# Cross-window attention on one core: QK, PV and output projection in 64x64 tiles of TensorE

## The chip, the cores and the metric

The kernel runs on one core of one Trainium2 chip. The core has five engines that run side by side and meet at semaphores: TensorE (matmuls, written PE, and its weight loads, PEld), VectorE (DVE), ScalarE (ACT), GpSimd (POOL) and the sync engine (SP), which here issues all transfers. TensorE writes only to PSUM, which has eight banks of 512 fp32 per partition; VectorE and ScalarE read from there, GpSimd does not. The metric is the time of one execution on the device in microseconds, lower is better, as the median of several runs. A profile of one execution gives the time of every instruction.

## What is computed

The input has 224 x 224 tokens of 96 channels in bf16. The first 48 channels of q, k and v attend within horizontal stripes of 8 rows, the last 48 within vertical stripes of 8 columns. Every stripe is a sequence of 1792 tokens, and there are 28 of each kind.

```python
def reference(x, wqkv, wo):
    B, H, W, C = x.shape                      # 1, 224, 224, 96
    qkv = jnp.einsum('bhwc,cd->bhwd', x, wqkv)
    q, k, v = (qkv[..., :C], qkv[..., C:2 * C], qkv[..., 2 * C:])
    scale = C2 ** (-0.5)                      # C2 = 48
    # horizontal stripes, first 48 channels
    ah = _softmax(jnp.einsum('bqc,bkc->bqk', qh, kh) * scale, axis=-1)
    oh = jnp.einsum('bqk,bkc->bqc', ah, vh)
    # vertical stripes, last 48 channels
    av = _softmax(jnp.einsum('bqc,bkc->bqk', qv, kv) * scale, axis=-1)
    ov = jnp.einsum('bqk,bkc->bqc', av, vv)
    o = concat(oh, ov)
    return jnp.einsum('bhwc,cd->bhwd', o, wo)
```

## The kernel before

Two stripes of one kind make a pair, called P in the code: P = 0 to 13 are horizontal, 14 to 27 vertical. The two stripes of a pair (w = 0, 1) lie on partitions 0 to 63 and 64 to 127. The kernel holds Q and K transposed (channels on partitions, 48 of 64 used) and V with tokens on partitions and a column of ones behind the 48 channels, so that PV also gives the sum of the row. A row's maximum is not taken; the mean of K over the stripe is subtracted instead, which changes nothing in the softmax.

**Loads and fills.** `load(P)` (L383) puts x transposed into one of two buffers `xT_sb`: a horizontal stripe is one transposing DMA, a vertical one is eight of 224 tokens, so a vertical P takes 16. A buffer is free when all the fills of the P two before have read it. `prep(P)` (L478) projects it in 12 fills: K and Q in four chunks of 512, 512, 512 and 256 tokens, V in two parts for each stripe. A fill is a matmul group into one PSUM bank and a VectorE evacuation (L518 for K with its sum, L513 for Q, L555 for V); GpSimd subtracts the mean of K (L529). The fills of P + 1 are spread over the time of P.

**Units.** For every P and every chunk of 512 queries there are 14 key tiles of 128 tokens (7 double tiles for the chunk of 256). Such a unit is QK (L708): two matmuls, one for each stripe, 48 rows by 128 columns by 512, side by side in the two row halves of the array, each into a bank of its own. So a unit is a 128 x 1024 tile of scores in a pair of banks. Of 49 units of a P, 41 go to ScalarE, which takes the exponential of the tile in one instruction (L726, into one of eight buffers `PT`). The other 8 go to VectorE, which builds the exponential from the bits of the exponent in four instructions: I (L750, from PSUM), U (L756), E (L758) and G (L760); their product is a sum of two terms, E and G, so such a unit has two PV. PV (L691) is two matmuls for each unit, 128 rows by 64 columns by 512, one for each stripe, side by side in the two column halves of the array, added up over the key tiles in one bank.

**Banks.** Banks 0 to 5 are a ring of three pairs for scores. Banks 6 and 7 are accumulators for PV, taken by whichever chunk comes next. A fill or a projection takes one bank: a half of a ring pair, or an accumulator that is free (`FillPool`, L309).

**The end of a chunk.** VectorE copies the accumulator to `OT_sb` (L655), and `fin` (L565) projects it with `wo`: 128-row matmuls against a `wo` with zeros in the rows of the other stripe (L583 horizontal, L612 vertical). VectorE takes the reciprocal of the sum (L571) and multiplies: a horizontal result is kept in `Ph_sb` (L590), a vertical one goes to `tmp` (L619), GpSimd adds the horizontal part (L623), and four or two tiles for each stripe are stored, 28 stores in all for a P (L632).

**The order.** A planner in the kernel (`Planner`, L76) places all operations on all engines by its own table of costs and writes each engine's program in that order; each engine's program, the queue of SP included, is then fixed. `pick_pe` (L148) chooses TensorE's next operation. A change between the shape of the QK tiles and that of all others is a change of TensorE's mode. A wait that is late at the head of an engine's program holds all that stands behind it.

## Time and profile before

| | |
|---|---|
| median of 3 runs | 1107.05 us (1104.41 to 1108.44) |
| the profiled execution | 1103.27 us |
| its span, first to last instruction | 1101.5 us |
| mean granted clock of TensorE | 0.989 |
| exponentials on ScalarE (L726) | 1148, 1059.3 us busy |
| units on VectorE (L750) | 224 |
| stores / transposing loads of x | 392 / 252 |

How to read the views. A group line gives the source line, the engine, the operation, the tiles written and read with their shape, the count, then the busy time, the mean duration of one in ns, the idle time of the engine just before such instructions and what ended it. In the timeline a row has start, length, engine, line, operation and count, and in brackets the idle time before it and its releaser. "SPq" rows are the issue of transfers by the sync engine. "issue" as a releaser means that the profile shows nothing that the engine waited for; waits for a transfer appear so. Instructions of one engine overlap in part, so a mean duration is longer than the distance from one to the next.

### The profile page before, as it was taken

Reading aid. Unit: us, or ns where it says so; the run is one execution under the profiler, and the core shown is the slowest. Engines: PE = TensorE matmul, PEld = TensorE weight load, DVE = VectorE, ACT = ScalarE, POOL = GpSimd, SP = SyncE. Lnnn points to the kernel's source line nnn. Section 1 sums busy time; section 2 is a strip of 40 time slices with the busy share of each in tenths; the row PEclk is TensorE's granted clock in tenths of the full one; section 3 lists DMA queues with packets and bytes.
Section 4 is the critical chain, followed back from the end, with each engine's and each line's share of the span. In section 5 each row is a group of like instructions: output and inputs, shape, how many; then the busy total and the mean of one; then the engine's idle time right before and its main releaser. Section 6 shows DMA issues by size and latency. Waiting matters only on the chain.

```text
span 1101.5 us, 24997 instructions
## 1 busy us (share of the span) xinstructions
PE 1046.9 (95%) x10424; PEld 386.4 (35%) x10424; DVE 949.9 (86%) x1941; ACT 1062.8 (96%) x1154; POOL 153.3 (14%) x143
## 2 busy tenths in 40 slices
PE   7999999999999999999999999999999999989996
PEld 2333333333333333333333333333333333323332
DVE  5899889889888998898899889988988978868876
ACT  4999999999999999999999999999999989979996
POOL 0000000000000000000022122222221222212221
PEclk9999999999999999999999999999999989989998
DMA  5101201110121012011112222222222222222110
GB/s 104 35 1 35 35 9 27 35 35 1 35 35 34 1 35 35 3 33 29 20 29 42 39 41 42 39 41 43 40 41 42 41 39 43 40 39 42 37 29 19
DMA packets 168904, 37.05 MB, mean 34 GB/s; under 512 B 168792, under 2 KB 168792, under 8 KB 168792
## 3 DMA queue, kind: packets, MB, share of 16 engines
q1 hardware_dynamic: 168792, 35.47, 17.5%
q8 instruction: 81, 1.33, 0.5%
q14 instruction: 31, 0.25, 0.1%
HBM read 0.10 MB, written 9.63 MB: 9 GB/s over the span
## 4 chain that ended last, share of the span: by engine, by line
ACT 63%; PE 17%; DVE 17%; issue 1%; DMA 0%; POOL 0%; POOLq 0%; SPq 0%
ACT PT L726 63%; PE ps L708 8%; PE ps L691 7%; DVE I_sb L750 5%; DVE G_sb L760 4%; DVE KT_sb L518 2%; DVE U_sb L756 2%; DVE E_sb L758 1%; DVE OT_sb L655 1%; PE ps L499 1%; PE ps L583 1%; DVE QT_sb L513 1%; DVE Ph_sb L590 1%; DMA xT_sb<-in_x_dram 0%; PE ps L612 0%
## 5 line engine op out<-in xcount | busy, mean ns | idle before, releaser
L726 ACT ACTIVATE PT<-ps 128x1024 bf16<-128x1024 f32 x1148 | 1059.3, 1107 | 20.8 <-PE ps L708 20.1
L708 PE MATMUL ps<-QT_sb,KT_sb 48*128 48x512 bf16 (+1 forms) x3136 | 490.9, 360 | 25.4 <-ACT PT L726 16.0
L691 PE MATMUL ps<-PT,V_sb 128*64 128x512 bf16 (+1 forms) x2576 | 447.6, 371 | 0.3 <-ACT PT L726 0.3
L750 DVE TENSOR_SCALAR I_sb<-ps 128x1024 int16<-128x1024 f32 x224 | 273.4, 1221 | 42.7 <-PE ps L708 37.7
L708 PEld LDWEIGHTS ps<-QT_sb,KT_sb 48*128 48x128 bf16 x3136 | 125.1, 93 | 327.8 <-ACT PT L726 195.6
L691 PEld LDWEIGHTS ps<-PT,V_sb 128*64 128x64 bf16 x2576 | 134.1, 108 | 170.4 <-issue 160.4
L760 DVE TENSOR_TENSOR G_sb<-I_sb,U_sb 128x1024 bf16<-128x1024 bf16 x224 | 176.9, 790 | 3.3
L623 POOL TENSOR_TENSOR out_sb<-tmp,Ph_sb 128x384 bf16<-128x384 f32 (+1 forms) x112 | 99.8, 896 | 414.4 <-DVE tmp L619 338.9
L529 POOL TENSOR_SCALAR KT_sb<-KT_sb,negmean 128x1792 bf16<-128x1792 bf16 x27 | 53.3, 1976 | 529.8 <-DVE kjunk L523 529.7
L756 DVE TENSOR_SCALAR U_sb<-I_sb 128x1024 int16<-128x1024 int16 x224 | 96.5, 431 | 2.0
L691 PE MATMUL ps<-G_sb,V_sb 128*64 128x512 bf16 (+1 forms) x560 | 91.1, 356 | 5.7 <-DVE G_sb L760 4.9
L499 PE MATMUL ps<-xT_sb,w_sb 96*64 96x512 bf16 x448 | 84.4, 379 | 11.1 <-issue 10.8
L758 DVE TENSOR_SCALAR E_sb<-I_sb 128x1024 int16<-128x1024 int16 x224 | 92.7, 414 | 0.0
L691 PE MATMUL ps<-E_sb,V_sb 128*64 128x512 bf16 (+1 forms) x560 | 89.6, 350 | 1.5 <-DVE E_sb L758 0.9
L518 DVE TENSOR_SCALAR_CACHE_REDUCE KT_sb<-ps 128x512 bf16<-128x512 f32 x112 | 68.3, 618 | 22.2 <-PE ps L499 22.0
L555 DVE CAST V_sb<-ps 128x480 bf16<-128x480 f32 x112 | 53.8, 501 | 38.2 <-PE ps L550 37.3
L513 DVE TENSOR_SCALAR QT_sb<-ps 128x512 bf16<-128x512 f32 x108 | 66.9, 619 | 18.2 <-PE ps L499 18.1
L655 DVE CAST OT_sb<-ps 128x512 bf16<-128x512 f32 x112 | 69.3, 618 | 6.8 <-PE ps L691 6.8
L619 DVE TENSOR_TENSOR tmp<-ps,rc 128x384 f32<-128x384 f32 (+1 forms) x112 | 56.3, 502 | 1.0
L590 DVE TENSOR_TENSOR Ph_sb<-ps,rc 128x384 bf16<-128x384 f32 x98 | 54.1, 552 | 0.6
L691 PEld LDWEIGHTS ps<-G_sb,V_sb 128*64 128x64 bf16 x560 | 27.0, 108 | 56.1 <-DVE G_sb L760 39.2
L571 DVE RECIPROCAL rc<-ps 128x4 f32<-128x4 f32 (+1 forms) x210 | 36.3, 173 | 10.3 <-PE ps L612 10.3
(28 smaller groups left out, 281.6 us busy)
## 6 DMA issues: line engine op xcount, KB each, us to landing
out_dram<-out_sb SPq DMA_DIRECT2D x392, 24.0 KB, 1.9
xT_sb<-in_x_dram SPq DMA_TRANSPOSE x252, 2.5
wo_sb<-in_wo_dram SPq DMA_DIRECT2D x4, 9.0 KB
wo_sb<-one_sb SPq DMA_DIRECT2D x4, 0.0 KB
w_sb<-in_wqkv_dram SPq DMA_DIRECT2D x1, 54.0 KB, 2.5
xT_sb<-in_x_dram SPq DMA_DIRECT2D x2, 3.0 KB, 3.9
```

The lines of the kernel that those rows point to most:

```text
L499: ins = e.matmul(bk[64 * w:64 * w + 64, 0:qs], lhsT=w_sb[0:C, wblk(P, kind), :], rhs=rhs, start=True, stop=True)
L513: return e.tensor_scalar(dst, src, A128, None, ALU.mult)
L518: return e.tensor_scalar(KT_sb[b][:, q0:q0 + qs], bk[:, 0:qs], 1.0, None, ALU.mult, ALU.add, accum_out=ksum[b][:, c:c + 1])
L623: return e.tensor_tensor(out_sb[b][:, w, g[0]:g[0] + n, :], tmp[hold[1].tok["t"]][:, 0:n, :], Ph_sb[:, g[0]:g[0] + n, j, :], ALU.add)
L655: return e.tensor_copy(OT_sb[b][:, q0:q0 + qs], bk[:, 0:qs])
L691: ins = e.matmul(bank(k.bank)[64 * w:64 * w + 64, 0:qs], lhsT=lhs(w, kt), rhs=rhs(w, i, qs), start=(op.tok["first"] and i == 0), stop=(k.l ...
L708: ins = e.matmul(bank(2 * s + w)[:, i * qs:(i + 1) * qs], lhsT=KT_sb[b][64 * w:64 * w + C2, kt * 128:(kt + 1) * 128], rhs=QT_sb[b][64 * w: ...
L726: a.fn = lambda e: e.activation(PT[a.tok["p"]][:].rearrange("p (s n) -> p s n", s=2), two(q.tok["s"]), ACTF.Exp, scale=LN128)
L750: d.fn = lambda e: e.tensor_scalar(I_sb[d.tok["y"]][:, :].rearrange("p (s n) -> p s n", s=2), two(q.tok["s"]), 128.0 * ONE, 0.0, ALU.add, ...
L756: f.fn = lambda e: e.tensor_scalar(U_sb[d.tok["y"]][:, :], I_sb[d.tok["y"]][:, :], M_FRAC, HALF, ALU.bitwise_and, ALU.bitwise_or)
L758: x2.fn = lambda e: e.tensor_scalar(E_sb[x2.tok["l"]][:, :], I_sb[d.tok["y"]][:, :], M_EXP, E_LOW, ALU.bitwise_and, ALU.bitwise_or)
L760: g.fn = lambda e: e.tensor_tensor(G_sb[x2.tok["l"]][:, :], I_sb[d.tok["y"]][:, :].bitcast(BF16), U_sb[d.tok["y"]][:, :].bitcast(BF16), AL ...
```

## The change

Two pairs, P = 2g and 2g + 1, now run side by side as the two lanes of a group g; there are 14 groups.

- QK is in 64 x 64 tiles: a unit has 64 keys of both stripes of both pairs against 512 queries of each, so four matmuls, which take the four quarters of the array. Lane p has bank p of the ring pair. PV is in 64 x 64 tiles as well, and so is the output projection, which now needs only the 49 rows of its own stripe (`wo_sb` has no zero half any more). The tile of a unit is 128 x 1024 as before.
- Each lane has an accumulator bank of its own, 6 or 7. The lanes go through their chunks in different orders (`ORDER`), so that one is at a chunk's end 14 units before the other; both end together at a group's end. Where one lane is in its chunk of 256 queries, the unit has six matmuls.
- A group has 98 units, 16 of them on VectorE, evenly spread (`dset`); 82 go to ScalarE.
- A fill or a projection takes a whole ring pair and is evacuated two banks at once: K in two fills of 896 tokens, Q in two, V in two, the projection in one for each chunk, up to 768 elements. At the start, K and half of Q of the second pair and half of Q of the first go through ScalarE.
- Q, K and V have four buffers instead of two; `xT_sb` still has two. The output goes through six buffers of one chunk, `tmp` through two.
- The fills of the next group are spread over the whole group, first those of its first pair, then those of the second.
- `pick_pe` is rewritten: there are two modes, the 64 x 64 tiles ("m") and the fills ("f"). At most two ring pairs are held for ScalarE while something else could take the third.

In the built program SP's order in the vertical half is, from the first store on: 12 stores, the 16 loads of P = 18, 32 stores, 16 loads, 24 stores, 16 loads and so on in turn, the 16 of P = 27, then 124 stores.

```diff
-    NKT = NTOK // 128
+    NKT = NTOK // 64
+    ORDER = [(0, 1, 2, 3), (3, 0, 1, 2)]
+    NG = NP // 2
...
-        wo_sb = [[sb(f"wo_sb{v}{w}", [128, C + 1], BF16) for w in range(2)] for v in range(2)]
+        wo_sb = [sb(f"wo_sb{v}", [128, C + 1], BF16) for v in range(2)]
-        QT_sb = [sb(f"QT_sb{i}", [128, NTOK], BF16) for i in range(2)]
-        KT_sb = [sb(f"KT_sb{i}", [128, NTOK], BF16) for i in range(2)]
-        V_sb = [sb(f"V_sb{i}", [128, 2, NKT, CP], BF16) for i in range(2)]
+        QT_sb = [sb(f"QT_sb{i}", [128, NTOK], BF16) for i in range(4)]
+        KT_sb = [sb(f"KT_sb{i}", [128, NTOK], BF16) for i in range(4)]
+        V_sb = [sb(f"V_sb{i}", [128, NKT, CP], BF16) for i in range(4)]
...
-        obanks = Pool([6, 7])
+        obank = [Pool([6]), Pool([7])]
...
     def pick_pe(s, cands):
+        t = s.t["pe"]
+        left = max(s.t["act"], t) + 0.903 * s.pend - t
+        mine = s.pend + sum(1 for f in s.ring.free_by.values() if f and f[0].eng == "act" and f[0].end > t + SLACK)
+        if mine >= MOST and any(q and p in (R_QD, R_FIN, R_FILL) and s.open(q[0]) for p, q in s.streams["pe"]):
+            cands = [c for c in cands if c[1] != R_QA]
+            if not cands:
+                return None
+        elif mine < MOST and any(p == R_QA for _, p, _ in cands):
+            cands = [c for c in cands if c[1] not in (R_QD, R_FIN, R_FILL)]
...
+            dset = {int((i + DOFF) * n / ND) for i in range(ND)}
+            for i, u in enumerate(zip(*lanes)):
+                units.append((g, i, i in dset, u))
...
         def fill(occ, pe_fn, pe_deps, evs, ...):
-            p = Op("pe", occ, occ + 0.18, lambda e: pe_fn(e, bank(p.tok["b"])), pe_deps, soft, [(fills, "b", 1)], mode="v")
+            p = Op("pe", occ, occ + 0.18, lambda e: pe_fn(e, p.tok["s"], p), pe_deps, soft, [(ring, "s", 1)], mode=mode)
...
         def prep(P, pace=None, startup=False):
+            for f in range(2):
+                def pe_fn(e, s, op, f=f):
+                    for i in range(2):
+                        for w in range(2):
+                            t0 = f * HF + i * HB
+                            ins = e.matmul(bank(2 * s + i)[64 * w:64 * w + 64, 0:HB], lhsT=w_sb[0:C, wblk(P, "k"), :],
+                                           rhs=xT_sb[xb][0:C, w, t0:t0 + HB], start=True, stop=True)
+                    return ins
+                def ev_fn(e, s, op, f=f):
+                    dst = KT_sb[b][:, f * HF:(f + 1) * HF].rearrange("p (i n) -> p i n", i=2)
+                    if startup and par:
+                        return e.activation(dst, two(s)[:, :, 0:HB], ACTF.Copy, accum_out=ksum[b][:, f:f + 1])
+                    return e.tensor_scalar(dst, two(s)[:, :, 0:HB], 1.0, None, ALU.mult, ALU.add, accum_out=ksum[b][:, f:f + 1])
...
+            put_q(halves[0], startup)
+            put_v(0)
+            put_v(1)
+            put_q(halves[1], False)
...
         def fin(k):
...
+                ins = e.matmul(bank(2 * s + i)[64 * w:64 * w + 64, j * (C + 1):(j + 1) * (C + 1)],
+                               lhsT=OT_sb[ot][64 * w:64 * w + CA, t0:t0 + 64], rhs=wo_sb[0][64 * w:64 * w + CA, :],
+                               start=True, stop=True)
...
         def pv_op(u, rhs, deps, then):
+            def fn(e):
+                todo = inter([[(k, kts, i, w) for i in range(len(kts)) for w in range(2)] for k, kts in u])
+                for k, kts, i, w in todo:
+                    r = w ^ k.p
+                    ins = e.matmul(bank(6 + k.p)[64 * w:64 * w + 64, 0:k.qs], lhsT=V_sb[k.P % 4][64 * r:64 * r + 64, kts[i], :],
+                                   rhs=rhs()[64 * r:64 * r + 64, k.p * 512 + i * k.qs:k.p * 512 + (i + 1) * k.qs],
+                                   start=(op.tok[k.p] and i == 0), stop=(k.last is op and i == len(kts) - 1))
+                return ins
...
+        def qk_op(u, soft, then):
+                for k, kts, i, w in todo:
+                    r = w ^ k.p
+                    b = k.P % 4
+                    ins = e.matmul(bank(2 * s + k.p)[64 * r:64 * r + 64, i * k.qs:(i + 1) * k.qs],
+                                   lhsT=KT_sb[b][64 * w:64 * w + C2, kts[i] * 64:(kts[i] + 1) * 64],
+                                   rhs=QT_sb[b][64 * w:64 * w + C2, k.q0:k.q0 + k.qs], start=True, stop=True)
...
         prep(0, startup=True)
+        prep(1, startup=True)
+        for g in range(NG):
...
+            if g + 1 < NG:
+                for p in range(2):
+                    load(2 * g + 2 + p, sp_in)
+                def pace():
+                    n = count[0]
+                    count[0] += 1
+                    return [act_of[a_idx[int((n + P0) * len(a_idx) * PACE / 12)]]]
+                for p in range(2):
+                    prep(2 * g + 2 + p, pace=pace)
```

## The prediction

> **What bounds the kernel now.** I read the busy totals first, then who ScalarE waited for by stretch, then the sync engine's queue, then both ends of the run.

> ```profile
> PE 1046.9 (95%) x10424; PEld 386.4 (35%) x10424; DVE 949.9 (86%) x1941; ACT 1062.8 (96%) x1154; POOL 153.3 (14%) x143
> 200.00:400.00 200.00, 193.39 (x1978) 73.46 (x1976) 176.35 (x357) 199.00 (x217) 10.88 (x5) 1.00 0.15 29
> 850.00:1000.00 150.00, 140.54 (x1314) 49.63 (x1312) 124.15 (x261) 138.28 (x150) 33.04 (x34) 0.94 0.21 41
> ```

> Columns of the two stretches: length, busy time of PE, PEld, DVE, ACT, POOL, granted clock, DMA share, GB/s. Two engines look full, but only ScalarE is: 199.00 us for 217 exponentials is 0.917 us each, and 1148 × 0.917 = 1053 us of the 1101.5 us span. TensorE's 95% counts latency and waits; most QK loads wait for an ACT slot (195.6 us on line 726). From 850 us on ScalarE loses 11.7 of 150 us, and the clock drops.

> ScalarE's idle time before L726, asked for 0 to 30 us, 30 to 850 us and 850 us to the end:

> ```profile
> ACT PT L726 <- PE ps L708: 3.7, 6, 1.4
> ACT PT L726 <- PE ps L708: 3.3, 16, 0.3
> ACT PT L726 <- PE ps L708: 13.1, 12, 3.1
> ```

> So 820 us in the middle hold 3.3 us of waiting: nothing done to TensorE or VectorE there can return more. The late 13.1 us have another source, the queue that issues all transfers:

> ```profile
> 583.84 21.42 SPq L397 DMA_TRANSPOSE xT_sb<-in_x_dram  x16
> 605.30 19.40 SPq L632 DMA_DIRECT2D out_dram<-out_sb  x28
> 891.41 16.59 SPq L632 DMA_DIRECT2D out_dram<-out_sb  x24
> 1014.88 84.84 SPq L632 DMA_DIRECT2D out_dram<-out_sb  x96
> 892.66 0.41 PE L499 MATMUL ps<-xT_sb,w_sb 96*64 96x512 bf16 x2 [2.30 <-issue]
> 893.66 1.94 ACT L726 ACTIVATE PT<-ps 128x1024 bf16<-128x1024 f32 x2 [2.24 <-PE ps L708]
> ```

> Columns: start, length, engine. In the vertical half each P needs 16 transposing loads (21.4 us of issuing) and 28 stores at 0.68 us (19.0): 40.4 us, against 41 × 0.917 = 37.6 us of exponentials. The queue falls 2.8 us behind per P, runs without a gap from 583.84 to 1014.88, and near 892 the K fill (L499) waits 2.30 us at the head of TensorE's order for its x. Then matmul pairs come 0.43 us apart instead of 0.22 until about 900 (clock row 0.69 for 890 to 900). The rest follows the queue: the last strip lands near 1017 (1013.49 + 1.34 + 2.4), 82 exponentials remain, 1017 + 75 = 1092, and the last exponential ends at 1093.68.

> **The change part by part.** Work that does not change: 1148 exponentials of 128x1024, 224 units on VectorE, 392 stores, 252 transposes. ScalarE's floor stays 1053 us.

> *Four 64x64 tiles.* A unit is now four matmuls (six where a 256-wide chunk takes part): in the built order 17,144 matmuls instead of 10,424, and 315 changes of tile shape instead of 1,956. No row shows four tiles at once, so bounds. Low 0.22 us per unit, as now; high 0.43, if the pairs run one after the other. What is nearest:

> ```profile
> 301.65 0.60 PE L708 MATMUL ps<-QT_sb,KT_sb 48*128 48x512 bf16 x4
> 316.26 0.64 PE L708 MATMUL ps<-QT_sb,KT_sb 48*128 48x256 bf16 x8 [0.19 <-ACT PT L726]
> 307.90 0.50 PE L550 MATMUL ps<-w_sb,xT_sb 96*64 96x48 bf16 x20
> ```

> The same columns in twice the instructions cost 0.04 us for four more: 0.01 each. I take 0.24 per unit. A change of shape costs 0.09 us (301.34 start of a 64-column pair, 0.22 of streaming, 301.65 the QK). Saved: 1,641 × 0.09 = 148 us; added: 6,720 × 0.01 = 67. Per group (two P, 75.2 us of exponentials): 212 units × 0.24 = 50.9, fills and projections about 7.4, shape changes 2: 60 us. All this lies beside ScalarE: worth 0. At the high end it is 91 + 9 = 100 us per group and the bound: + 25 × 14 = 350 us.

> [...]

> *Wide evacuations.* By shape, 512 to 256 elements is 684 to 419 ns for K (L518), 384 to 192 is 553 to 351 for the product (L619), 480 to 192 is 649 to 352 for V (L555). Continued: K and Q of 896 take 1.08, V of 672 0.85, the product of 768 0.96 us. Against today's counts VectorE saves about 1.7 us of 34 per P. ScalarE's exponentials cover it: worth 0; were VectorE the bound it would be 28 × 1.7 = 48 us.

> *The ring.* Fills lose the half slots and the spare accumulator banks; each takes a whole pair, and ScalarE keeps two of three. The third carries per group: 16 VectorE units (0.42 + 1.22 + 0.1 = 1.74), 8 K/Q fills (0.60 + 1.08 + 0.1), 4 V fills (0.63 + 0.85 + 0.1), 6 wide projections (0.54 + 0.18 + 0.96 + 0.1) and 2 narrow (1.2): 61 us, with 0.2 of queueing on 36 uses 68 us. VectorE's other 30 us (U, E, G, OT) must fit gaps of about 29 us in that loop; if a third doesn't, 78. Bounds 68 and 78 against 75.2. I take a fit, with 2 us lost in the horizontal half, since VectorE is at 88% there now and ScalarE still at 99.5%. One accumulator bank per lane: its 0.69 us evacuation delays the lane's next PV, behind which a QK may stand in TensorE's order; ScalarE holds up to 0.9 us of finished QK, and PV has eight PT buffers: 0. Six output buffers of 9 to 13 us of work each outlast a queue that is 25 us late: 0.

> *Start.* The first unit needs two P.

> ```profile
> 2.18 8.22 SPq L397 DMA_TRANSPOSE xT_sb<-in_x_dram  x4
> 9.20 2.56 PE L499 MATMUL ps<-xT_sb,w_sb 96*64 96x512 bf16 x12 [4.38 <-issue]
> 14.93 1.02 ACT L726 ACTIVATE PT<-ps 128x1024 bf16<-128x1024 f32 x1 [1.36 <-PE ps L708]
> ```

> Issues are 2.05 us apart; the second strip let PE go at 9.20, so the fourth comes near 13.2. Then, at pairs of 0.43: K 0.95, K and Q through ScalarE (0.9 each, in line) to 17.0, V fills in TensorE's order to 17.7, QK 0.65: first exponential 18.3, + 3.4 us. Bounds: +1.5 (strips earlier) and +5.

> *Queue of stores and loads.* The same 80.8 us per group, but a buffer is free 0.60 group (45 us) before its next use, with nothing between the 16 loads. In the new order load 18 can go 33 us into the vertical half, then 10 loads and 256 stores follow without a gap: 214 + 174 = 388, landing 2.5: x of P=27 is there at 423.5. From its place 122 exponentials remain: 112 us, plus 2 for the slow clock: the half takes 537.5. Without that wait, 574 × 0.917 + 2 = 529. Before: 573 exponentials have begun by 548 us and 575 by 550, so the half runs from 549.4 to 1093.7: 544.3. Gain 7. Bounds: 15 (queue keeps up) and −1 (2% slower issuing). It also covers the ring: losses under 8 us in this half vanish behind it.

> *End.* The last two chunks finish together, one 512 wide.

> ```profile
> 1095.14 0.42 DVE L655 CAST OT_sb<-ps 128x256 bf16<-128x256 f32 x1 [0.51 <-PE ps L691]
> 1096.68 1.05 POOL L623 TENSOR_TENSOR out_sb<-tmp,Ph_sb 128x192 bf16<-128x192 f32 x2 [2.59 <-DVE rc L571]
> ```

> From the last exponential: PV 0.45, two OT casts to 1.45, projections, reciprocals and products to 3.3, GpSimd 1.6 (0.55 to 0.91 us for 192 to 384, continued) to 5, then 8 stores × 0.6 behind 4, landing: 12 instead of 7.8. + 4.2, bounds + 2 and + 6.

> **Sum.** 1101.5 + 3.4 + 2 − 7 + 4.2 = 1104, with the 1.8 us outside the span 1106 against that execution's 1103.3. The median of the runs is 3.8 above that execution; I add nothing, since late loads make that scatter and fewer are late: 1106, range of this case 1098 to 1113.

> **Rivals.** *The queue keeps up:* ScalarE never waits for x in the vertical half: 8 us less, 1098; with a start of + 1.5 1096. For it: 45 us of notice instead of 44, less 3 for four stores that no longer split the loads. Against: 5.6 us per group lost over five groups. *The third slot binds:* the loop passes 75.2 us per group; U, E and G run late, G's PV and the next D unit come late, projections pile up, the next group's K is late. At 77 us: 1.8 × 14 = 25, less 8 covered: 1123; at 78, 1137. It decides from about 76. For it: one slot where halves used to overlap. Against: VectorE's total falls. *Tiles run in pairs, not fours:* the change does not do what it says; 1106 + 350.

> **Chances.** About 0.5% is what can be told from no change: faster below 1101.5, slower above 1112.6. Forecast 0.45 (a seventh of it on each outer side), queue keeps up 0.25, third slot 0.25, pairs 0.05. Faster 0.06 + 0.25 = 0.31, slower 0.06 + 0.25 + 0.05 = 0.36, same the remaining 0.33. The range leaves out the fastest ends of the second case and the pairs and worst loops: 1095 to 1130.

> **What would show it.** Right: 0.917 us per exponential between 200 and 400 us; units 0.24 us apart with changes of shape rare; PE busy well down, yet the time unmoved; first exponential near 18.3; the store queue without gaps after the first vertical group; 12 us after the last exponential. [...] Wrong: ScalarE waiting in the horizontal half (ring), or four matmuls starting 0.2 us apart (pairs).

## The result and the profile after

The changed kernel takes 1123.49 us in the median of four runs (1122.51 to 1125.59), the kernel before, on the same chip, 1107.74 us (1104.41 to 1110.67): a ratio of 1.0146, 95% interval 1.0113 to 1.0178. It is slower by about 1.5%; the forecast was 1106 us and no change. The profiled execution took 1122.51 us with a span of 1120.7.

The page of the changed kernel, busy time of each engine and the queue that the page calls instruction (packets, MB, share of the 16 DMA engines' time), and that queue in the page of before:

```profile
PE 970.8 (87%) x17144; PEld 431.6 (39%) x17144; DVE 919.8 (82%) x1522; ACT 1063.0 (95%) x1156; POOL 129.3 (12%) x86
...
q8 instruction: 134, 2.20, 0.8%
...
q8 instruction: 81, 1.33, 0.5%
```

TensorE is busy 76 us less, VectorE 30 less, and ScalarE just as long: the tiles do what they were to do, and what the kernel loses is time in which ScalarE waits. The same two stretches as before, same columns:

```profile
200.00:400.00 200.00, 181.29 (x3234) 81.40 (x3232) 171.50 (x281) 199.71 (x219) 8.79 (x5) 1.00 0.15 27
850.00:1000.00 150.00, 122.24 (x2200) 55.27 (x2196) 115.99 (x190) 133.10 (x144) 25.79 (x17) 0.94 0.22 40
```

In the horizontal half ScalarE does two exponentials more than before in 200 us. In the late stretch it loses 16.9 of 150 us, against 11.7 before. ScalarE's waits for L675 (QK), for 0 to 30 us, 30 to 850 us and 850 us to the end (us in total, times, longest):

```profile
ACT PT L699 <- PE ps L675: 2.9, 4, 1.2
ACT PT L699 <- PE ps L675: 9.9, 3, 9.0
ACT PT L699 <- PE ps L675: 16.6, 7, 8.9
```

Three waits hold nearly all of it: 9.0, 6.4 and 8.9 us, at 818, 904 and 987 us, one a group. The first of them on TensorE and on ScalarE in the timeline:

```profile
816.81 0.39 PE L675 MATMUL ps<-QT_sb,KT_sb 48*64 48x512 bf16 x4
825.76 0.96 PE L442 MATMUL ps<-xT_sb,w_sb 96*64 96x448 bf16 x4 [8.56 <-DMA xT_sb<-in_x_dram]
826.64 0.64 PE L675 MATMUL ps<-QT_sb,KT_sb 48*64 48x512 bf16 x4
827.07 0.64 PE L651 MATMUL ps<-E_sb,V_sb 64*64 64x512 bf16 x4
...
827.34 1.02 ACT L699 ACTIVATE PT<-ps 128x1024 bf16<-128x1024 f32 x1 [8.99 <-PE ps L675]
```

The first K fill of an odd P (L442) stands at the head of TensorE's program and waits 8.56 us for its x; all QK and PV stand behind it. After it the units are 0.43 us apart instead of 0.22 for a while. The queue that issues the transfers, in the vertical half:

```profile
584.30 21.74 SPq L342 DMA_TRANSPOSE xT_sb<-in_x_dram  x16
606.09 24.65 SPq L596 DMA_DIRECT2D out_dram<-out_sb  x32
630.84 22.71 SPq L342 DMA_TRANSPOSE xT_sb<-in_x_dram  x16
653.60 17.23 SPq L596 DMA_DIRECT2D out_dram<-out_sb  x24
...
755.61 23.66 SPq L342 DMA_TRANSPOSE xT_sb<-in_x_dram  x16
...
993.31 17.21 SPq L596 DMA_DIRECT2D out_dram<-out_sb  x26
```

It is full from 584.30 to the end of the last load at 993.3: 409 us for the ten loads and 256 stores that the prediction put at 388. A group of 32 loads and 56 stores takes some 85 us of issuing against 75.7 us of exponentials (82 times 0.923 us, the mean distance in this half without ScalarE's waits). Why issues take longer than they did is to be seen in the chain of waits, where each issue has its own row (start, length, what):

```profile
806.53 1.24 SPq L342
807.77 0.04 issue
807.81 2.15 SPq L342
809.96 0.04 issue
810.00 1.24 SPq L342
...
817.71 1.66 SPq L342
...
823.26 2.41 DMA xT_sb<-in_x_dram
825.67 0.09 issue
825.76 0.96 PE ps L442 x4
```

A load takes 1.24 us to issue, a store 0.60, nearly all alike to a few ns, but some, here called long, take 0.3 to 1.3 us more. The two long ones here lie where the trace has packets of 16,384 bytes on the instruction queue q8, at 807.97 (0.96 us) and 817.38 (0.95). Its packets follow TensorE's program: the 81 in the page of before are 63.7 bytes for each of 20,848 instructions (10,424 matmuls and as many weight loads), the 134 in the page above 64.0 for each of 34,288. From these two counts I estimate that the queue brings TensorE its program, at 64 bytes an instruction, and a packet on it is called a fetch here. With 15,436, 19,888 and 11,992 matmuls, in the runs below, the estimate gives 120.6, 155.4 and 93.7 packets, and their pages count 120, 155 and 94. Between 584 and 1000 us all 31 long issues of the kernel before and 49 of the 50 of the changed one overlap such a fetch in time; the last one starts 0.4 us after a fetch. The other issues are no slower than before.

### The profile page after: what moved, and what is told of

Same layout as the page of the kernel before. It is cut to its first block, busy times and chain, and to the rows that moved or that the text cites. A ratio compares the mean times of both kernels' runs of the same rounds, so it can differ in the third digit from the quotient of the medians.

```text
span 1120.7 us, 37910 instructions
## 1 busy us (share of the span) xinstructions
PE 970.8 (87%) x17144; PEld 431.6 (39%) x17144; DVE 919.8 (82%) x1522; ACT 1063.0 (95%) x1156; POOL 129.3 (12%) x86
## 4 chain that ended last, share of the span: by engine, by line
ACT 66%; issue 10%; DVE 9%; PE 8%; SPq 3%; POOL 2%; DMA 1%; POOLq 0%
ACT PT L699 66%; SPq L342 3%; DVE I_sb L709 3%; PE ps L675 3%; PE ps L651 2%; DVE G_sb L718 2%; POOL out_sb L587 2%; DVE QT_sb L491 1%; PE ps L477 1%; PE ps L442 1%; DMA xT_sb<-in_x_dram 1%; DVE OT_sb L630 1%; DVE U_sb L714 1%; DVE E_sb L716 1%; DVE tmp L584 1%
## 5 line engine op out<-in xcount | busy, mean ns | idle before, releaser
L699 ACT ACTIVATE PT<-ps 128x1024 bf16<-128x1024 f32 x1148 | 1057.7, 1097 | 32.1 <-PE ps L675 29.4
L675 PE MATMUL ps<-QT_sb,KT_sb 48*64 48x512 bf16 (+1 forms) x6272 | 534.0, 364 | 32.6 <-ACT PT L699 16.2
L651 PE MATMUL ps<-PT,V_sb 64*64 64x512 bf16 (+1 forms) x5264 | 440.0, 358 | 52.8 <-ACT PT L699 40.6
L675 PEld LDWEIGHTS ps<-QT_sb,KT_sb 48*64 48x64 bf16 x6272 | 192.7, 105 | 276.4 <-ACT PT L699 203.0
L651 PEld LDWEIGHTS ps<-PT,V_sb 64*64 64x64 bf16 x5264 | 183.0, 106 | 201.9 <-ACT PT L699 157.7
L587 POOL TENSOR_TENSOR out_sb<-tmp,Ph_sb 128x768 bf16<-128x768 f32 (+1 forms) x56 | 83.4, 1489 | 350.4 <-DVE tmp L584 350.4
L651 PE MATMUL ps<-E_sb,V_sb 64*64 64x512 bf16 (+1 forms) x1008 | 90.5, 365 | 8.0 <-DVE OT_sb L630 7.4
L651 PE MATMUL ps<-G_sb,V_sb 64*64 64x512 bf16 (+1 forms) x1008 | 88.1, 358 | 2.9 <-DVE G_sb L718 2.8
L450 DVE TENSOR_SCALAR_CACHE_REDUCE KT_sb<-ps 128x896 bf16<-128x896 f32 x54 | 58.8, 1091 | 37.0 <-PE ps L442 34.0
L630 DVE CAST OT_sb<-ps 128x256 bf16<-128x256 f32 (+1 forms) x112 | 68.1, 618 | 9.2 <-PE ps L651 8.2
L491 DVE TENSOR_SCALAR QT_sb<-ps 128x896 bf16<-128x896 f32 x54 | 58.7, 1086 | 2.9 <-PE ps L477 0.9
L442 PE MATMUL ps<-xT_sb,w_sb 96*64 96x448 bf16 x224 | 34.6, 395 | 28.3 <-DMA xT_sb<-in_x_dram 23.0
```

The lines of the kernel that those rows point to most:

```text
L450: return e.tensor_scalar(dst, two(s)[:, :, 0:HB], 1.0, None, ALU.mult, ALU.add, accum_out=ksum[b][:, f:f + 1])
L491: return e.tensor_scalar(dst, src, A128, None, ALU.mult)
L587: return e.tensor_tensor(out_sb[op.tok["o"]][:, :, 0:n, :], tmp[hold[1].tok["t"]][:, :, 0:n, :], Ph_sb[:, k0:k0 + n, j0:j0 + 2, :].rearran ...
L630: return e.tensor_copy(OT_sb[k.evac.tok["ot"]][:, 0:k.qs], bank(6 + k.p)[:, 0:k.qs])
L651: ins = e.matmul(bank(6 + k.p)[64 * w:64 * w + 64, 0:k.qs], lhsT=V_sb[k.P % 4][64 * r:64 * r + 64, kts[i], :], rhs=rhs()[64 * r:64 * r + 6 ...
L675: ins = e.matmul(bank(2 * s + k.p)[64 * r:64 * r + 64, i * k.qs:(i + 1) * k.qs], lhsT=KT_sb[b][64 * w:64 * w + C2, kts[i] * 64:(kts[i] + 1 ...
```

## The experiments

Theory A: the vertical half is set by SyncE's issue queue, by late x. Theory F, within it: the queue got slower because each fetch of TensorE's program that meets an issue holds it up, and the change has more program. Rival B: the tiles, the ring or the evacuations cost the time. Rival C: not the queue's pace but its order, stores ahead of loads. Spans of the profiled executions: before 1101.5, changed 1120.7 us. Every ratio is to the kernel before on the same chip; a span is that of one execution, and those of the kernel before scatter (its times lie between 1102.2 and 1112.1 us).

**Half of the stores on another queue.** The stores of the second stripe of each pair (w = 1) go to GpSimd's queue: 196 of the 392, all of them in the vertical half, and not 196 in each half as the expectation has it. This is done in the changed kernel, and in the same way in the one before (where a copy into an output buffer then also waits for both queues' stores from it):

```diff
-  dm = Op("sp", 0.06, 2.0, lambda e, w=w, j=j: e.dma_start(...), [op], dma=(s_out[o_], 0))
-  sp_out.append(dm)
+  dm = Op("pool" if w else "sp", 0.06, 2.0, lambda e, w=w, j=j: e.dma_start(...), [op], dma=((s_outp if w else s_out)[o_], 0))
+  (pool_o if w else sp_out).append(dm)
```

> The changed kernel, with the stores of the second sequence of each pair issued by GpSimd's queue instead of SyncE's: 196 in the horizontal half and 196 in the vertical one, under semaphores of their own. Theory A (SyncE's queue bounds the vertical half: 10 transposing loads and some 256 stores take it 409 us, and TensorE waits three times for an x that was issued too late): the three waits of L442 at odd P are gone, ScalarE waits for nothing longer than 1 us between 550 and 1080 us, the vertical half takes 531 to 535 us instead of 558, and the span is 1093 to 1097 us, 24 to 28 less. Theory B (the 64x64 tiles, the ring of banks or the wide evacuations cost the time themselves): the span stays at 1118 to 1122 us.

> The kernel before with the same edit. Theory A: the kernel before also waited for loads in its vertical half, but less: 544 us becomes 531 to 535, and the span 1088 to 1092 us. What is left between this run and the changed kernel with the same edit is then what the tiles, the start and the end cost without the queue: 3 to 9 us by the longer end (12.4 against 7.8 us). Theory B: between the two runs lie the same 16 us as between the two kernels.

Measured: the changed kernel with the edit 1098.53 us, ratio to the kernel before 0.9937 (0.9922 to 0.9952), span 1096.9; the kernel before with the edit 1095.07 us, 0.9906 (0.9891 to 0.9921), span 1093.0. The second is 1 us above the expected 1088 to 1092. ScalarE's waits from 550 to 1080 us, first of the changed kernel with the edit, then of the kernel before with it:

```profile
ACT PT L700 <- PE ps L676: 0.2, 1, 0.2
ACT PT L727 <- PE ps L709: 2.2, 6, 0.5
```

Without the edit they are 26.3 and 12.5 us; the waits for x are gone. The last exponential ends at 1080.4 us in the one kernel and at 1080.2 in the other: with the queue out of the way the two tilings are equal up to there, although the first exponential begins 4.2 us later in the changed one, and B falls. What lies between them, 3.9 us, is the end. Both ends are some 4 to 5 us longer than without the edit (16.5 and 12.8 us), which the next pair of runs takes up.

**The last stores back on SyncE's queue.** As above, but for the last two pairs all stores stay on SyncE's queue (`w and P < NP - 2`).

> The changed kernel with the second sequences' stores on GpSimd's queue except those of the last two pairs, which stay on SyncE's. In the run with all of them on GpSimd's queue, the last exponential ended at 1080.4 and the kernel 16.5 us later, in the changed kernel 12.6 us after it. If GpSimd's queue lengthens the end: 1080.4 + 12.6, span 1092 to 1094 us. If not: 1096 to 1098 us.

> The kernel before with the same edit. Last exponential at 1080.2 with all second stores on GpSimd's queue, and the end 12.8 us after it; in the kernel before the end was 7.8 us after the last exponential. If GpSimd's queue lengthens the end: 1080.2 + 7.8, span 1087 to 1089 us, the fastest of all. If not: 1092 to 1094 us.

Measured: 1094.38 us, ratio 0.9878 (0.9848 to 0.9908), span 1093.3, end 12.6 us; and 1091.31 us, 0.9847 (0.9812 to 0.9883), span 1089.8, end 9.2 us, a little over the 1087 to 1089 expected. So stores on GpSimd's queue lengthen the end. Both are faster than both kernels, and the old tiles with the relieved queue are the fastest: the change still costs its longer end.

**The order of the queue.** The loads' stream stands ahead of the stores' one, and the planner is told the costs of issues.

```diff
-        sp_out, sp_in = (pl.stream("sp", i) for i in range(2))
+        sp_in, sp_out = (pl.stream("sp", i) for i in range(2))
...
+                    op.occ = 2.05 if is_h[P] else 1.35
...
-                        dm = Op("sp", 0.06, 2.0, lambda e, w=w, j=j: ...
+                        dm = Op("sp", 0.7, 2.4, lambda e, w=w, j=j: ...
```

> The changed kernel with the same DMAs on the same queue, but the loads put ahead of the stores where both are due, and the planner told what an issue costs (1.35 us a vertical load, 2.05 a horizontal one, 0.7 a store). Theory A in the form 'the loads stand behind stores that could wait': six output buffers let the stores lag, the loads come in time, and the span is 1094 to 1100 us. Theory A in the form 'the queue has more to issue than time for it': 84 us of issues to a group of 76 us; stores fall back until the output buffers are full, the waits move from x to the output copies, and the span is 1112 to 1122 us. Theory B: 1118 to 1122 us.

> The kernel before with the same edit of order and planned issue costs. It has only two output buffers, so stores can lag by little. If order is what matters: span 1090 to 1096 us. If the queue's throughput is what matters: 1098 to 1106 us, as before.

Measured: the changed kernel 1113.53 us (span 1111.4, 9 less), the kernel before 1118.88 us (span 1116.8, 15 more). No expectation holds to the number: order, with the costs the planner is told, recovers 9 of the 24 us that relief recovers, and in the kernel before it is harmful, which I had not expected. What GpSimd waited for from 550 to 1080 us, first in the changed kernel with the edit (us in total, times, longest):

```profile
POOL out_sb L588 <- DMA out_dram<-out_sb: 95.0, 14, 18.7
```

and in the kernel before with it:

```profile
POOL out_sb L624 <- DMA out_dram<-out_sb: 115.8, 6, 42.4
```

Neither kernel has such a wait without the edit. Stores fall back until the output buffers are full; six of them soften it (ScalarE's longest wait is 4.8 us), two don't (14.3 us). The queue has too much to issue, in whichever order; C is no more than a part.

**More program for TensorE.** An extra matmul of 8 columns, written over by the next one, adds program (155 packets on q8 instead of 134) and little work (2.3 us of span with the relieved queue, see below). It was put into the vertical half, into the vertical half of the version with the relieved queue, and into the horizontal half:

```diff
+                    if i == 0 and k.P >= NPH:
+                        e.matmul(bank(2 * s + k.p)[64 * r:64 * r + 64, 0:8], lhsT=KT_sb[b][...], rhs=QT_sb[b][...], start=True, stop=True)
                     ins = e.matmul(bank(2 * s + k.p)[64 * r:64 * r + 64, i * k.qs:(i + 1) * k.qs],
```

> The changed kernel with one extra matmul of 8 columns in front of each tile's first QK matmul, in the vertical half alone (the real one writes the same place after it): about 2744 matmuls and as many weight loads more, 351 KB of program, which is some 21 more of the 16 KB fetches. Theory F (each fetch of TensorE's program holds up one DMA issue of SyncE by about 0.77 us, and the queue has no time to spare): some 20 fetches lie in the time that the queue sets, so 14 to 17 us more, span 1133 to 1139 us; the long issues between 584 and 1000 us rise from 50 to about 65. Without F, and TensorE 87% busy: 1119 to 1123 us. If the extra TensorE work itself counts, about 0.1 us for each of some 1372 units of exponentials... the same sum would then show in the next run too.

> The same extra matmuls in the changed kernel whose second sequences' stores are issued by GpSimd's queue, where SyncE's queue has time to spare. Theory F: as many more fetches and long issues, but nothing waits for them: span 1096 to 1099 us, as without the extra matmuls (1096.9). If the extra work on TensorE costs by itself, the span rises here as in the run before.

> The changed kernel with the extra matmuls of 8 columns in the horizontal half alone. Theory F: as many more fetches (155 against 134), but in a half in which no load or store is late; only the issues from the 12th group on count: span 1119 to 1124 us, against 1131.9 with the same matmuls in the vertical half. If the matmuls cost by themselves: some 2 to 3 us more, as the run with the relieved queue showed (1099.2 against 1096.9), so 1123 to 1124; if it were any 21 fetches wherever they fall: 1131.

**Less program.** The other direction, with the same transfers. In the vertical half this kernel leaves out PV of one stripe of each pair but for a chunk's first and last tile, so it computes something else:

```diff
                     r = w ^ k.p
+                    if k.P >= NPH and w == 0 and not (op.tok[k.p] and i == 0) and not (k.last is op and i == len(kts) - 1):
+                        continue
                     ins = e.matmul(bank(6 + k.p)...
```

> The changed kernel with part of the computation left out: in the vertical half PV leaves out the first sequence of each pair except the first and the last key tile of a chunk, some 1700 matmuls and weight loads less, 217 KB of program or 13 fetches, and the same DMAs. Theory F: about 12 fewer long issues between 584 and 1000 us, 9 to 10 us off the queue's 409.0 us, waits of ScalarE for x shorter, span 1109 to 1113 us. Without F, and TensorE not the bound: 1119 to 1122 us.

Measured, with the queue's stretch from the first issue of the tenth load from the last to the end of the last one, which is the same 160 load issues and 256 stores in each kernel of this tiling (252 in the kernel before). "Regular" is every issue at 1.241 or 0.598 us, "excess" what the issues take beyond that; the gaps between them, with one short issue of 0.58 us, sum to 19.7 or 19.8 us in all five:

| kernel | fetches on q8 | of them in the stretch | stretch | regular | long issues | excess | span |
|---|---|---|---|---|---|---|---|
| before | 81 | 29 | 390.0 us | 349.3 | 29 | 21.1 us | 1101.5 |
| changed, less program | 120 | 39 | 399.3 | 351.6 | 39 | 27.9 | 1110.7 |
| changed | 134 | 49 | 409.0 | 351.6 | 50 | 37.6 | 1120.7 |
| changed, more in the horizontal half | 155 | 48 | 406.8 | 351.6 | 49 | 35.4 | 1119.3 |
| changed, more in the vertical half | 155 | 64 | 419.4 | 351.6 | 64 | 47.9 | 1131.9 |

The medians are 1113.33 us (less program; ratio 1.0075, 1.0043 to 1.0107), 1122.34 (more, horizontal; 1.0152, 1.0119 to 1.0185) and 1134.6 (more, vertical; 1.0244, 1.0209 to 1.0278), where the changed kernel has 1.0146 (1.0113 to 1.0178). Program added or taken away in the vertical half moves the stretch by +10.4 and −9.7 us and the span by +11.2 and −10.0; the same program in the horizontal half, where no load is late, moves them by −2.2 and −1.4, no more than the spread between executions of one kernel (3.1 us of the changed one). With the relieved queue the extra matmuls cost 2.3 us (median 1100.94 us, span 1099.2 against 1096.9, a little over the 1096 to 1099 expected): where no x is late, their own work costs no more than that. These five kernels agree with F: a long issue costs some 0.75 us, and the stretch changes by the excess and by next to nothing else. The expected 1133 us and more was a little high, since the stretch has 14 long issues more and not 20.

**The same on the kernel before.** An 8-column matmul in front of each QK matmul of its vertical half:

> The kernel before with an extra matmul of 8 columns in front of each QK matmul of its vertical half, 1568 in all, 201 KB of program or 12 fetches more. Theory F: its queue, too, has no time to spare between 624 and 1015 us (the period of its loads is 40.6 us against 37.9 of exponentials), so some 11 of the 12 fetches at 0.77 us count: 7 to 9 us more, span 1108 to 1111 us. Without F: up to 3 us for the work on TensorE, span 1101 to 1105 us.

Measured: 1117.91 us, ratio 1.0114 (1.0068 to 1.0159), span 1114.9, 13.4 more, and more than either expectation. The stretch grew by 7.5 us (397.5; excess 28.5 against 21.1), as F has it. Of the 13.4 us, 7.9 are there at the end of the last load's issue, 4.7 come between that and the last exponential, 0.8 at the end. The 4.7 go with a late x as well: the first K fill of the last P, first in the kernel before and then with the extra matmuls, and ScalarE in the latter:

```profile
1016.73 0.41 PE L499 MATMUL ps<-xT_sb,w_sb 96*64 96x512 bf16 x2
1024.53 0.64 PE L499 MATMUL ps<-xT_sb,w_sb 96*64 96x512 bf16 x2 [1.66 <-issue]
1026.22 2.16 ACT L729 ACTIVATE PT<-ps 128x1024 bf16<-128x1024 f32 x2 [2.38 <-PE ps L711]
```

The kernel before has no wait there. With the extra matmuls the clock granted to TensorE is 0.50 from 1024.4 to 1034.6 us, and ScalarE waits 2.4, 1.0 and 1.7 us, at 1023.8, 1028.4 and 1033.6 us. Whether the extra work also counts by itself, in a kernel whose TensorE is busy 95% of the time, stays open; single executions lie between 1112.91 and 1124.81 us.

## Why the prediction was wrong

The bound was named rightly: ScalarE everywhere, and SyncE's queue in the vertical half. By the steps of the prediction:

- **Tiles.** 0.24 us a unit, beside ScalarE, worth 0: right. Units of four in the changed kernel:

```profile
304.42 0.39 PE L675 MATMUL ps<-QT_sb,KT_sb 48*64 48x512 bf16 x4
304.64 0.39 PE L651 MATMUL ps<-G_sb,V_sb 64*64 64x512 bf16 x4
304.86 0.38 PE L651 MATMUL ps<-PT,V_sb 64*64 64x512 bf16 x4
```

  These start 0.22 us apart (0.24 in the median of the units that follow one another between 100 and 540 us), so the rival of pairs falls: four weight loads with two tiles to a row group fit into the 0.22 us.
- **Evacuations.** K and Q took 1.09 us (1.08 forecast), the product of 768 elements 0.96 (0.96); VectorE saved 30 us, worth 0 as said.
- **Ring.** The 2 us forecast for the horizontal half were not there: ScalarE has no wait on QK between 30 and 550 us. The third slot does not bind; that rival gave 1123 us, near the time measured, by a mechanism that is not there. That the stated range of 1095 to 1130 us takes in the measured 1123.49 is owed to it, and is luck.
- **Start.** The first exponential began at 19.47 us, not 18.3. But what a late start and the ring were to cost, 5.4 us, was nearly all regained: the 575th exponential began at 549.7 us against 549.1 before, since ScalarE's gaps up to there sum to 2.5 us instead of 5.3, and the mean distance without them is a little shorter.
- **Queue: the step that failed.** "In the new order load 18 can go 33 us into the vertical half, then 10 loads and 256 stores follow without a gap: 214 + 174 = 388". The order was right, and so were the missing gaps, the place (584.3 us is 34.6 us into the half) and what follows the last load: 112 us plus 2 forecast, and 113.0 measured from the K fill that this load let go, at 995.11, to the end of the last exponential. The price of an issue was wrong. Regular issues and gaps make 371.4 us, so 388 holds 16.6 us of long issues. The same stretch of the kernel before holds 21.1 (my rows were low by 4.5), and the changed kernel 37.6: 16.5 more, because 49 fetches of its TensorE program fall into the same stretch, and 29 of the kernel before. The sum of the two is the 21 us of 409 − 388. I took a price from the kernel before as a constant of the queue, and the change itself moved it: the prediction counted 6,720 matmuls more as worth 0 beside ScalarE, and did not ask what else their instructions use. So the half took 558.5 us and not 537.5, and the gain of 7 us was a loss of 13.9. "2% slower issuing" was my outer bound; it was 5%.
- **End.** 12 us forecast, 12.6 measured, from the last exponential at 1108.15 to 1120.73.

The sum with what was measured: 1101.5 + 0.5 (up to the 575th exponential) + 13.9 (vertical half, forecast −7) + 4.8 (end) = 1120.7. This is for the two profiled executions, which lie 19.2 us apart; the medians lie 15.8 apart, since the profiled execution of the kernel before, 1103.27 us, is faster than all four that make its median. What its slower executions lose, no trace shows. Of the 13.9, ScalarE's gaps are 14.3 us more (28.4 against 14.1), and its exponentials a little closer. The queue costs both kernels time in the vertical half: with it relieved, the last exponential ends 27.8 us earlier in the changed kernel and 13.4 in the one before.

"Queue keeps up" was the rival with the right question and the wrong sign: 45 us of notice for a load instead of 44 weighs little when the queue falls 9 us behind per group.

## What to carry to other kernels

When a change multiplies the instructions of an engine, price its program too: here 6,720 matmuls more cost next to nothing on TensorE and 16.5 us on another engine's queue. A price read in the rows before holds only while what lies beside it stays, so split it into its regular part and its exceptions and ask what makes the exceptions. A queue that is full over a whole stage is worth more than the tiling around it: moving half of the stores away took 28 us from the last exponential of one kernel and 13 from that of the other.

## What the runs showed of the hardware

Stores issued from GpSimd's queue made the end longer by 3.6 and 3.2 us of span in the two tilings (1096.9 against 1093.3, 1093.0 against 1089.8). The cause was not looked into.

The clock granted to TensorE fell to 0.50 after gaps on TensorE of 2.30 us and 3.14 us in the kernel before (at 893.8 and 975.7 us), within those of 8.56, 5.93 and 8.48 us in the changed one (at 818.6, 907.3 and 989.2 us), and it was 0.50 from 1024.4 us on, at the end of a gap of 1.66 us, with the extra matmuls in the kernel before. It stayed at 1.00 after one of 0.96 us (kernel before, to 933.96 us). Which length of gap decides, or whether the length alone does, these runs do not show.
